# An HGRN2 recurrence with a PReLU network on one core: the first four steps as 735 single operations in a new order, and the usual steps without their column product

## The chip, the core and the metric

The kernel runs on one core of a Trainium2 chip. A core has TensorE (PE in the profile, with PEld for its weight loads), VectorE (DVE), ScalarE (ACT), GpSimd (POOL) and SyncE (SP), each with its own list of instructions, worked off in order and held up by semaphores. Data comes from HBM through DMA engines; a transfer is issued by SP, ACT or POOL, and an issue that waits holds up whatever stands behind it on that engine. The metric is the device time of one execution in microseconds (us).

## What is computed

```python
def _attn_ref(q, k, v, f_logit):                    # B, H, S, D = 4, 8, 768, 48
    f = 1.0 / (1.0 + np.exp(-f_logit))
    state = np.zeros((B, H, D, D))
    for t in range(S):
        state = f[:, :, t, :, None] * state + np.einsum('bhd,bhe->bhde', k[:, :, t], v[:, :, t])
        y[:, :, t] = np.einsum('bhd,bhde->bhe', q[:, :, t], state)

def _moe_ref(x, w_in, w_out, alpha):                # x: 3072 x 384, d_ff 2048
    h = x @ w_in
    g = np.maximum(h, 0.0) + alpha * np.minimum(h, 0.0)
    return g @ w_out
```

A recurrence over 768 times gives `y` for four batches of eight heads, and a network with one hidden layer of 2048 is applied to each of the 3072 rows.

## The kernel before

**Steps.** Time is cut in six chunks of 128 (`C`), the batches in two pairs (`U` = 2), which makes 12 steps: step 0 is pair 0 in chunk 0, step 1 is pair 1 in chunk 0, step 2 is pair 0 in chunk 1, and so on. A step has three parts. `preparation` loads f, q, k and v (token `ld`), applies the sigmoid (`sg`), and makes products of neighbouring factors (`l1` to `l3`, into `kr`, `fs` and `qd`), two scans (`sc`), and scaled queries and keys (`le`, `k4`, `e2` to `e7`; in the first chunk `gk`, `nr`; `ke`, `sa`, `sb`). From chunk 1 on, the keys are turned on VectorE (`kt`) and moved by 16 transfers on SP (`km`) into `ksn`; in chunk 0 TensorE transposes them (`kp`, copied by `kc`). `attention` makes score products (`r`, `x`, in chunk 0 also `h`, in blocks of 4, 16 and 32 times), copies them under masks into `ad` (`R`, `X`, `H`), from there into `A` (`p00` to `p13`), adds products with later keys (`of`, `oc`) and the state's columns (`s00` to `s11`), updates the state (`pd`, `m0`, `m1`, in step 0 also `pz`), and multiplies `A` with values and state (`y0`, `y1`), copied by `z0`, `z1`. The output goes into the layout of the network by transfers (`mv`), in step 0 by products with `dense` (`t0`, `t1`, copied by `T00` to `T12`). `network` multiplies by `w_in` (`n`), takes the negative part on ScalarE (`g`) and the sum on VectorE (`G`), and multiplies by `w_out`: in step 0 plainly (`va`, `vb`, result `o0`, `o1`), in the others by seven half-size products instead of eight (`A1`, `B`, `C1`, `D`, `A2`, `C2`, `E`), whose sums `S0`, `S1` are taken first.

**Weights.** `w_in` and `w_out` come as 64-bit words in eight pieces each (`id`, `jd`), through five staging buffers; ScalarE makes an upper and a lower part (`ih`, `il`, `jh`, `jl`), and a 16-bit sum on VectorE joins them (`ib`, `jb`). The first network products of step 0 (`na0`: batch a, hidden columns 0 to 511) need pieces 0 and 1.

**Order.** The order of all instructions is written out: `FIRST` lists tokens `word:step` for the first four steps (network of step n beside preparation of later steps), and `USUAL` is repeated for steps 4 to 12, where a `-` is the step before and a `+` the step behind. Each engine takes its instructions in this order. A letter at the end of a token chooses the engine: V or G for VectorE or GpSimd in `elementwise` (line 211), A or V for copies, V or A for the queue of a weight load.

**The column product** (`kw`, line 641) is a product of one column of `ident` with four columns of `ksn`. It waits for all 16 key moves, so that the state products (`pd`, line 635) behind it need no such waits. Its target is the bank that the network product `n3` then overwrites (`phk` in the profile). In `USUAL` it stands ahead of `n3`, and `pd` behind `of`.

**Memory.** PSUM holds pairs of banks (`psa`, two of them) for scores, offsets, state and output, and single banks for keys, layout and network (`psn`, four). `f`, `q`, `k` have one buffer each over the steps.

```python
def keys_landed():
    to = ahead[n - 1, 3] = bank(f"phk_{i}")
    nc.tensor.matmul(to[0:1, 0:4], lhsT=ident[:, 0:1], rhs=x["ksn"][:, 0, 0:128:32], start=True, stop=True,
                     skip_group_check=True)
```

Of the kernel before, what the change touches and what calls it, by code (L numbers as in the profile page):

```python
# [33 lines left out]
ldb:0 lda:0 id3V:0 id0V:0 id5V:0 id4V:0 id1V:0 sgb:0 qcb:0 l1bV:0 l2bV:0 l3bV:0 scb:0 c0b:0 sga:0 qca:0 l1aV:0 l2aV:0 l3aV:0 krb:0 sca:0 k4bV:0 fs:0  # L34
c1b:0 c2b:0 c3a:0 kra:0 c2a:0 c1a:0 c0a:0 cgb:0 c3b:0 ih3:0 cga:0 leaV:0 lebV:0 ih0:0 C:0 bl:0 ld:1 k4aV:0 gkaV:0 gkbV:0 nrbV:0 keaV:0 kebV:0 nraV:0
r1:0 r0:0 h0:0 H0:0 il5:0 ih5:0 h1:0 il3:0 il0:0 ih4:0 H1:0 il4:0 saaV:0 sabV:0 R0:0 ib0:0 x1:0 kpa:0 x0:0 kpb:0 sg:1 kca:0 kcb:0 R1:0 X0:0 qc:1
p01A:0 p03A:0 p02A:0 p00A:0 ih1:0 l1V:1 ib5:0 id7V:0 id6V:0 jd5V:0 id2V:0 sbaG:0 s11a:0 s10a:0 sbbG:0 s11b:0 bl:1 l2V:1 X1:0 l3G:1 pzb:0 pza:0 pda:0
pdb:0 m0a:0 ofb:0 ofa:0 oc0a:0 oc1a:0 y0:0 z0V:0 t0:0 p12G:0 p11G:0 p13G:0 p10G:0 oc1b:0 oc0b:0 il1:0 sc:1 il6:0 m0b:0 ih6:0 T01A:0 T00A:0 s10b:0 y1:0
ld:2 ib1:0 jl5:0 jh5:0 T02V:0 ib4:0 ib3:0 ib6:0 na0:0 z1A:0 il2:0 ih2:0 t1:0 cg:1 c2:1 T10A:0 c1:1 c3:1 ga0:0 c0:1 ih7:0 T11A:0 T12A:0 kr:1 m1:0 jb5:0
ib2:0 jd1V:0 jd0V:0 jd4V:0 jd2V:0 jd3V:0 leV:1 r0:1 r1:1 na2:0 nb2:0 jl1:0 jl0:0 ga2:0 k4V:1 gkV:1 saV:1 na1:0 il7:0 jl4:0 sg:2 h1:1 h0:1 H0:1 qc:2  # L40
ga1:0 Ga0:0 Ga2:0 sbV:1 ib7:0 nb0:0 jd7V:0 jd6V:0 kr:2 jl2:0 H1:1 jh4:0 gb0:0 nb3:0 gb3:0 jl3:0 jh2:0 jh0:0 nrG:1 R0:1 Ga1:0 R1:1 Gb0:0 keV:1 Gb3:0
x1:1 x0:1 nb1:0 kp:1 X1:1 X0:1 l1G:2 s10:1 l2G:2 l3G:2 k4G:2 p03G:1 s11:1 p01G:1 p13G:1 p11G:1 p02G:1 p12G:1 p10G:1 c1:2 c2:2 gb1:0 gb2:0 jh1:0 kc:1
Gb2:0 r1:2 pd:1 of:1 na3:0 c3:2 m0:1 oc0:1 oc1:1 p00A:1 c0:2 R1:2 y0:1 jb4:0 fs:1 jb1:0 jb0:0 jb2:0 jh6:0 jl6:0 jh7:0 y1:1 r0:2 jh3:0 ga3:0 z0A:1
z1A:1 jl7:0 mv:1 Gb1:0 jb3:0 leV:2 e2G:2 e3G:2 ld:3 m1:1 Ga3:0 sc:2 jb7:0 keV:2 fs:2 e4V:2 jb6:0 L:0 kt:2 e5G:2 e6G:2 R0:2 e7V:2 W00V:0 va0:0 va1:0
va2:0 n0:1 vb0:0 vb1:0 sg:3 qc:3 g0:1 l1G:3 l2V:3 saV:2 sbG:2 va3:0 x0:2 x1:2 vb2:0 G0:1 n7:1 vb3:0 n6:1 km:2 pd:2 of:2 kw:2 n5:1 n3:1 X1:2 W01V:0
# [10 lines left out]
r0 R0 x0 X0 n0- g0- G0- n1- g1- G1- r1 R1 x1 X1 n2- g2- G2- kw n3- g3- G3- S0- of oc0 oc1 pd m0 n4- g4- G4- ld+ sg+ kr+ qc+ l1+ l2+ l3+ c0+ c1+ c2+  # L56
# [25 lines left out]
def kernel(  # L82
# [65 lines left out]
    nc.scalar.dma_start(out=lvl, in_=masks)  # L148
    nc.scalar.dma_start(out=om, in_=alpha)


    vs = []
    for bp in range(B // U):
        vs.append(const.tile([128, NC2, U, DM + 16], F32, tag=f"vs{bp}", name=f"vs{bp}"))
        nc.vector.memset(vs[bp], 0.0)

    kr = const.tile([128, W // 4, 4], F32, tag="kr", name="kr")
    nc.gpsimd.memset(kr[:, :, 3:4], 1.0)
    NS = G * (NB + 1) + 1
# [18 lines left out]
    nc.gpsimd.memset(ad, 0.0)  # L178
# [3 lines left out]
    nc.gpsimd.memset(A, 0.0)  # L182
# [3 lines left out]
    def constants():  # L186
        make_identity(nc, ident)
        nc.gpsimd.tensor_scalar(om, om, -1.0, 1.0, ALU.mult, ALU.add)
        nc.gpsimd.memset(mhalf, 0.0)
        for half in range(2):  # L190
            for m in range(1, NQ):
                n = NQ - m
# [4 lines left out]
        for par in range(2):  # L197
            nc.gpsimd.tensor_copy(dense[:, (2 + par) * D:(3 + par) * D], ident[:, 64 * par:64 * par + D])
# [790 lines left out]
```

## Time and profile before

| | |
|---|---|
| time, three runs | 616.82, 619.78, 620.09 us (median 619.78) |
| span of the profiled execution | 613.4 us, clock 0.999 |
| PE, PEld, DVE, ACT, POOL busy | 96%, 86%, 79%, 40%, 18% of the span |
| instructions | 18759 |

The time of the profiled execution itself is not listed beside its span; the three runs lie 3.4 to 6.7 us above that span. The page lists busy time by engine, the chain of work that ended last, and groups of equal instructions; the trace behind it also gives stretches of the span, waits by what ended them, and instructions in order of time. In a row such as `PE L717 MATMUL xt<-y,dense` stand the engine, the line, the operation, and the target and sources by the program's tile names, without buffer numbers. "x12" counts records; a 32-bit product leaves two. PE's ends are modelled.

### The profile page before, as it was taken

How to read it: one execution, taken by the hardware profiler on the slowest of the kernel's cores; microseconds unless marked ns; L12 is line 12 of the kernel's file. 1: busy time of each engine (PE TensorE's matmuls, PEld its weight loads, DVE VectorE, ACT ScalarE, POOL GpSimd, SP SyncE). 2: the span in 40 equal slices, each digit the busy share in tenths (PEclk: the TensorE clock that was granted, in tenths of full speed). 3: DMA queues.
4: the chain of work that ended last, by engine and by line, in shares of the span. 5: the costliest groups of instructions: out<-in, count | busy, mean ns of one | idle time of the engine just before them, and what ended most of it. 6: DMA issues, size and time to landing. Idle time of an engine off the chain costs nothing.

```text
span 613.4 us, 18759 instructions
## 1 busy us (share of the span) xinstructions
PE 586.4 (96%) x8042; PEld 526.6 (86%) x8042; DVE 485.3 (79%) x993; ACT 242.5 (40%) x464; POOL 109.5 (18%) x154
## 2 busy tenths in 40 slices
PE   1689899999999999999999999999999999999997
PEld 1589766898999799899899899889899889889997
DVE  7988899985588789799899799789799889762251
ACT  5887732523412352361272271361362263223110
POOL 7437566298050000000000000000000000000000
PEclk9999999999999999999999999999999999999999
DMA  8996343141002502502502502502602601201000
GB/s 272 322 337 186 103 142 53 41 136 24 14 25 45 153 10 43 158 2 49 161 1 50 159 2 47 162 2 42 168 1 39 162 11 35 47 2 27 26 1 26
DMA packets 72002, 50.40 MB, mean 82 GB/s; under 512 B 47248, under 2 KB 62480, under 8 KB 71920
## 3 DMA queue, kind: packets, MB, share of 16 engines
q1 hardware_dynamic: 64464, 38.77, 23.6%
q0 software_dynamic: 2944, 8.59, 4.8%
q10 hardware_dynamic: 4512, 1.85, 1.2%
q8 instruction: 63, 1.03, 0.8%
q14 instruction: 19, 0.16, 0.1%
HBM read 36.21 MB, written 4.72 MB: 67 GB/s over the span
## 4 chain that ended last, share of the span: by engine, by line
PE 84%; DVE 6%; ACT 3%; issue 2%; POOL 2%; DMA 2%; POOLq 0%; ACTq 0%; DVEq 0%
PE ph L763 32%; PE pc L859 10%; PE pa L859 9%; PE pe L859 5%; PE pd L859 5%; PE pb L859 5%; PE py L694 4%; PE phk L763 4%; PE qu L514 3%; PE raw L493 3%; DMA q<-in_qT 2%; PE ph L781 2%; PE state L635 2%; PE off L597 1%; DVE w_out_sb L211 1%
## 5 line engine op out<-in xcount | busy, mean ns | idle before, releaser
L763 PE MATMUL ph<-xT,w_in_sb 128*128 128x256 f32 x948 | 213.0, 382 | 0.0
L763 PEld LDWEIGHTS ph<-xT,w_in_sb 128*128 128x128 f32 x948 | 177.7, 190 | 27.0 <-issue 1.7
L769 ACT ACTIVATE neg<-ph 128x512 f32<-128x512 f32 x79 | 46.3, 597 | 146.7 <-PE ph L763 110.7
L773 DVE SCALAR_TENSOR_TENSOR gate<-neg,om,ph 128x256 f32<-128x256 f32 x158 | 67.7, 476 | 40.5 <-ACT neg L769 39.5
L731 POOL DMA_DIRECT2D xT<-y x22 | 11.9, 546 | 392.0 <-ACT y L703 392.0
L859 PE MATMUL pa<-w_out_sb,gate 128*128 128x192 f32 x352 | 61.9, 328 | 0.1
L859 PE MATMUL pc<-t,S 128*128 128x192 f32 x352 | 61.7, 329 | 0.0
L859 PEld LDWEIGHTS pa<-w_out_sb,gate 128*128 128x128 f32 x352 | 57.9, 190 | 2.0 <-DVE gate L773 1.3
L859 PEld LDWEIGHTS pc<-t,S 128*128 128x128 f32 x352 | 57.3, 190 | 0.8 <-issue 0.2
L522 DVE COPY_PREDICATED ad<-mquad,qu 128x224 f32<-128x224 int32 (+6 forms) x140 | 42.0, 300 | 9.3 <-PE qu L514 3.2
L501 DVE COPY_PREDICATED ad<-mraw,raw 128x256 f32<-128x256 int32 (+1 forms) x96 | 42.4, 441 | 7.0 <-POOL A L680 2.8
L345 ACT COPY ut<-qd 128x256 f32<-128x256 f32 (+1 forms) x52 | 32.0, 634 | 23.2 <-DVE qd L211 12.1
L211 DVE TENSOR_TENSOR ut<-ut,fs 128x512 f32<-128x512 f32 (+6 forms) x64 | 38.5, 604 | 3.3 <-POOL ut L211 2.4
L429 ACT COPY A<-q 48x512 f32<-48x512 f32 x40 | 24.7, 616 | 35.2 <-DVE q L211 31.9
L882 ACT ACTIVATE o<-pa 128x192 f32<-128x192 f32 x11 | 3.6, 330 | 76.9 <-PE pa L859 76.9
L493 PE MATMUL raw<-qd,k 48*32 48x80 f32 x1536 | 22.4, 243 | 10.3 <-DVE qd L211 10.3
L493 PEld LDWEIGHTS raw<-qd,k 48*32 48x32 f32 x1536 | 18.1, 109 | 15.7 <-issue 15.5
L680 ACT COPY A<-ad 32x256 f32<-32x256 f32 x75 | 30.1, 401 | 1.1
L859 PE MATMUL pe<-w_out_sb,S 128*128 128x192 f32 x176 | 30.5, 327 | 0.0
L859 PE MATMUL pb<-t,gate 128*128 128x192 f32 x176 | 30.4, 326 | 0.0
L859 PE MATMUL pd<-w_out_sb,S 128*128 128x192 f32 x176 | 30.4, 326 | 0.0
L694 PEld LDWEIGHTS py<-A,vs 128*64 128x64 f32 x768 | 26.0, 145 | 4.0 <-issue 2.2
(138 smaller groups left out, 894.3 us busy)
## 6 DMA issues: line engine op xcount, KB each, us to landing
w_out_raw<-in_w_out SPq DMA_DIRECT2D x8, 767.8 KB, 5.5
w_in_raw<-in_w_in SPq DMA_DIRECT2D x8, 767.2 KB, 12.1
out<-o SPq DMA_DIRECT2D x24, 192.0 KB, 2.1
f<-in_fT SPq DMA_DIRECT2D x7, 512.0 KB, 4.3
q<-in_qT SPq DMA_DIRECT2D x7, 512.0 KB, 5.2
k<-in_kT SPq DMA_DIRECT2D x7, 512.0 KB, 6.9
vs<-in_v SPq DMA_DIRECT2D x14, 192.0 KB, 6.9
ksn<-kt SPq DMA_DIRECT2D x80, 32.0 KB, 2.0
```

Of the source, the lines that this page charges most:

```text
L211: (nc.gpsimd if beside[0] else nc.vector).tensor_tensor(*a)
L345: w[f"c{r}{mark}"] = lambda r=r: nc.scalar.copy(q4()[:, gs, :, r], qdv[r][:, gs, :, 0])
L429: copy(A[halves(cc)[1], u0:u1, par * HP:(par + 1) * HP, CH * cc:CH * (cc + 1)], x["q3"][rows(par)].rearrange("p (u h c) s t -> p u h c (s ...
L493: nc.tensor.matmul(to[DB * j:DB * (j + 1), par, hp * C:hp * C + QW], lhsT=x["k"][r_, g * DB:(g + 1) * DB], rhs=qd[r_, g], start=True, stop ...
L501: nc.vector.copy_predicated(adu[:, :, :, d:4], mraw[:, d, :, d:4].bitcast(I32).unsqueeze(1).broadcast_to((128, H, NB, n_)), rv[:, :, QO[d] ...
L522: nc.vector.copy_predicated(ad[:, u, :, :, 4 * m:DB], mquad[:, lo:lo + n_].bitcast(I32).unsqueeze(1).unsqueeze(1).broadcast_to((128, 2, HP ...
L680: copy(A[s_, u, :, s_], ad[s_, u].rearrange("p r h t -> p (r h) t"))
L694: nc.tensor.matmul(to[64 * par:64 * par + 64, u, o:o + CH], lhsT=vs[bp][:, cc, u, hd * D:hd * D + 64], rhs=A[:, u, par * HP + hp, CH * cc: ...
L763: nc.tensor.matmul(ph[f][:, j * T:(j + 1) * T], lhsT=w_in_sb[:, kt, m * 128:(m + 1) * 128], rhs=x["T"][:, kt], start=(kt == 0 and j == 0), ...
L769: nc.scalar.activation(neg[f], ph[f].rearrange("p (j t) -> p j t", j=2), AF.Relu, scale=-1.0)
L773: nc.vector.scalar_tensor_tensor(gate[:, m % NH, m // NH], neg[f][:, j], om[:, m:m + 1], ph[f].rearrange("p (j t) -> p j t", j=2)[:, j], A ...
L859: nc.tensor.matmul(p[name][:, 0:DH], lhsT=of(f), rhs=by(f), start=(f == 0 and not more), stop=(f == NH - 1), skip_group_check=True)
```

## The change

1. The set-up (clears and masks), the constants, and every group of operations that used to be one token become single tokens: `several(w, name, ops)` gives `name` for all and `name.0`, `name.1`, ... for each.
2. `FIRST` is written anew with these tokens: 735 in another order. Engines are chosen anew for each elementwise operation (for example `l1b.0G`: the first factor product of half b on GpSimd, `ib0V`: a weight sum on VectorE), and loads of f, q, k, v can go to SP (V), ACT (A) or GpSimd (G). Both halves' f and q are now loaded ahead of k and v. Step 2's f and q come from SP, between weight loads; before, GpSimd issued them.
3. Three "idle" products on a cleared part of `gate` are put in (`iq.8`, `ip.11`, `ix.8`), into the banks of `qu`, `py` and `xt0`, ahead of `r1:0`, `y0:0` and `t0:0`.
4. `kw` is taken out everywhere. In `USUAL`, `pd` moves from behind `oc0 oc1` to behind `n3 g3 G3 S0`, ahead of `of`. In `FIRST`, `pd:2` and `pd:3` stand ahead of `of` too.

```diff
 USUAL = """
-r0 R0 x0 X0 n0- g0- G0- n1- g1- G1- r1 R1 x1 X1 n2- g2- G2- kw n3- g3- G3- S0- of oc0 oc1 pd m0 n4- g4- G4- ld+ sg+ kr+ qc+ l1+ l2+ l3+ c0+ c1+ c2+
+r0 R0 x0 X0 n0- g0- G0- n1- g1- G1- r1 R1 x1 X1 n2- g2- G2- n3- g3- G3- S0- pd of oc0 oc1 m0 n4- g4- G4- ld+ sg+ kr+ qc+ l1+ l2+ l3+ c0+ c1+ c2+
...
+    def several(w, name, ops):
+        w[name] = lambda: [op() for op in ops]
+        for n, op in enumerate(ops):
+            w[f"{name}.{n}"] = op
...
-            def load():
-                loads = nc.gpsimd if 0 < n <= FROM else nc.sync
-                for name, src in (("f", fT), ("q", qT), ("k", kT)):
...
+            def loads():
+                return {"A": nc.scalar, "G": nc.gpsimd, "V": nc.sync}.get(letter[0], nc.gpsimd if 0 < n <= FROM else nc.sync)
...
+        def idle(to):
+            nc.tensor.matmul(to[:, 0:128], lhsT=gate[:, 0, 0, 0:128], rhs=gate[:, 0, 0, 128:256], start=True, stop=True,
+                             skip_group_check=True)
...
+            for mark, home in (("q", lambda: got("qu", psf)[:, 0]), ("k", lambda: got("pk", psf)[:, 0]),
+                               ("s", lambda: got("state")[:, 0]), ("p", lambda: got("py")[:, 0]), ("x", first_bank)):
+                several(w, f"i{mark}", [lambda home=home: idle(home()) for _ in range(32)])
```

The new list around the places that the prediction speaks of, first from the start to the first network product, then around the keys of step 1 and the first outputs of the network (left out: "..."):

```
zi:0 ms:0 al:0 ldb.0V:0 zd:0 zf:0 zA:0 zo.0:0 zv0:0 ci:0 zo.1:0 zm:0 mr.2:0 sgb:0 l1b.0G:0 zv1:0 ldb.1V:0 lda.0V:0 iq.8:0 qcb:0 lda.1V:0 c0b:0 ch.0:0
...
sbb.1G:0 R0.0:0 nra.1V:0 kca:0 nra.0G:0 nra.2G:0 il4:0 fs:0 cd.2:0 ld.4V:1 sg:1 ld.2V:1 cq.6:0 R0.1:0 sba.1G:0 qc:1 R0.2:0 R1.2:0 R1.3:0 x1:0 co:0
x0:0 s10a:0 ch.5:0 ch.1:0 R0.3:0 X1.0:0 X0.0:0 ofb:0 ofa:0 ch.2:0 X1.1:0 id7V:0 ih4:0 l1.0G:1 il1:0 X0.1:0 oc0a:0 s11a:0 oc1a:0 l2.0V:1 pzb:0 jd3V:0
ch.6:0 X0.2:0 p01V:0 p02V:0 p03V:0 ib5V:0 pza:0 pda:0 X1.2:0 pdb:0 m0a:0 oc0b:0 oc1b:0 p13V:0 ih1:0 cq.1:0 l3.0V:1 sc.0:1 cq.4:0 l1.1V:1 p00G:0 cg:1
p10A:0 jd2V:0 sbb.0G:0 s10b:0 ib0V:0 jd5V:0 s11b:0 ip.11:0 y0:0 ix.8:0 p12V:0 z0A:0 il3:0 ib3V:0 cd.1:0 p11A:0 bl:1 m0b:0 t0:0 T00A:0 ib1V:0 T01A:0
l2.1V:1 T02A:0 c0:1 y1:0 na0:0 il2:0 z1A:0 t1:0 ...
H1.0:1 ld.0V:2 ld.2G:2 jb5V:0 H1.2:1 sg:2 H1.1:1 ...
jh4:0 X1.1:1 jd6V:0 kp:1 X1.2:1 l2.1G:2 of:1 X0.1:1 X0.2:1 Gb1.3:0 p02V:1 jh0:0 Gb1.1:0 p11V:1 p12A:1 gb3:0 Gb3.2:0 p10A:1 p03A:1 ld.1V:4 l3.1G:2
p01V:1 r1:2 oc0:1 oc1:1 na3:0 p00G:1 kc:1 pd:1 jl7:0 l3.0G:2 r0:2 m0.1:1 m0.0:1 ...
ld.0V:3 jb6V:0 L:0 ld.4A:2 Ga3.0:0 vb0:0 sg:3 fs:1 va0:0 m1.0:1 sc.0:2 fs:2 saV:2 z0A:1 va1:0 mv:1 sb.1V:2 e2V:2 vb1:0 R0.2:2 m1.1:1 e3V:2 vb2:0 vb3:0
o1:0 ke.1V:2 ke.2G:2 e4G:2 e5V:2 va2:0 R0.3:2 kt:2 e6G:2 e7V:2 km:2 x1:2 x0:2 ...
```

More of the change, by code (lines that the diff above doesn't have):

```diff
@@ L147, with piece @@
     lvl = const.tile([128, 2, DB], F32, tag="lvl", name="lvl")
-    nc.scalar.dma_start(out=lvl, in_=masks)
-    nc.scalar.dma_start(out=om, in_=alpha)
+    pieces, ahead = {}, {}
+    def piece(name):
+        return lambda fn: pieces.__setitem__(name, fn)
+    piece("zi")(lambda: nc.gpsimd.memset(gate[:, 0, 0], 1.0))
+    piece("ms")(lambda: nc.scalar.dma_start(out=lvl, in_=masks))
+    piece("al")(lambda: nc.scalar.dma_start(out=om, in_=alpha))
     vs = []
@@ new lines @@
+    for n, (half, m) in enumerate((half, m) for half in range(2) for m in range(1, NQ)):
+        piece(f"ch.{n + 1}")(lambda half=half, m=m: half_mask(half, m))
+    piece("cd.0")(lambda: nc.gpsimd.memset(dense, 0.0))
+    for par in range(2):
+        piece(f"cd.{par + 1}")(lambda par=par: nc.gpsimd.tensor_copy(dense[:, (2 + par) * D:(3 + par) * D],
+                                                                     ident[:, 64 * par:64 * par + D]))
+    piece("cq.0")(lambda: nc.gpsimd.memset(mquad, 0.0))
```

313 lines of the change are left out of this document (157 added, 156 removed).

## The prediction, before the changed kernel had run

> **What bounds the kernel now.** I read the page first, then five stretches of the span, then the waits of TensorE.
>
> ```profile
> span 613.4 us, 18759 instructions
> PE 586.4 (96%) x8042; PEld 526.6 (86%) x8042; DVE 485.3 (79%) x993; ACT 242.5 (40%) x464; POOL 109.5 (18%) x154
> PE 84%; DVE 6%; ACT 3%; issue 2%; POOL 2%; DMA 2%; POOLq 0%; ACTq 0%; DVEq 0%
> ```
>
> ```profile
> 0.00:39.32 39.32, 20.26 (x501) 17.81 (x501) 32.36 (x74) 28.22 (x59) 22.81 (x59) 1.00 0.97 309
> 39.32:64.20 24.88, 24.87 (x504) 24.09 (x500) 22.63 (x43) 21.29 (x38) 13.46 (x15) 1.00 0.74 234
> 64.20:77.08 12.88, 10.13 (x321) 8.98 (x321) 9.82 (x26) 9.34 (x18) 5.91 (x9) 1.00 0.16 58
> 77.08:199.97 122.89, 122.38 (x1534) 104.40 (x1531) 99.58 (x196) 39.64 (x74) 58.72 (x55) 1.00 0.26 62
> 199.97:613.40 413.43, 408.72 (x5196) 371.37 (x5192) 320.90 (x658) 144.00 (x277) 8.60 (x16) 1.00 0.23 58
> ```
>
> The columns are the stretch, its length, then busy time of PE, PEld, DVE, ACT and POOL, the granted clock, DMA share and GB/s. TensorE sets the end: its products are the same ones before and after, so time can only come out of its idle time. That idle time is 39.32 - 20.26 = 19.1 us until the first network product, 2.75 us between 64 and 77, 0.5 until 200, and 4.7 behind it, the tail after the last product included. VectorE is the busy one while TensorE is idle at the start: 32.4 of 39.3 us.
>
> ```profile
> PE raw L493 <- DVE qd L211: 10.3, 2, 7.1
> PE raw L553 <- DVE ut L211: 3.4, 1, 3.4
> PE state L635 <- DVE ad L538: 3.4, 1, 3.4
> PE state L635 <- issue: 1.3, 1, 1.3
> PE keys L571 <- DVE ks L211: 1.2, 1, 1.2
> PE xt L717 <- DVE y L703: 0.9, 1, 0.9
> PE py L694 <- ACT A L616: 0.7, 1, 0.7
> ```
>
> Each row is waits in us, times, longest. The first three and the last two lie in the opening, the keys near 65, and the state wait at 207, in the first usual step.
>
> **The change part by part.** *The opening.* These rows are the end of TensorE's opening chain, and the same layout product later:
>
> ```profile
> 31.41 2.36 PE L694 MATMUL py<-A,vs 128*64 128x64 f32 x32 [0.70 <-ACT A L616]
> 34.64 2.90 PE L717 MATMUL xt<-y,dense 128*128 128x128 f32 x12 [0.88 <-DVE y L703]
> 37.46 1.92 PE L694 MATMUL py<-A,vs 128*64 128x64 f32 x32
> 39.32 0.94 PE L781 MATMUL ph<-xT,w_in_sb 128*128 128x128 f32 x6
> 42.10 1.50 PE L717 MATMUL xt<-y,dense 128*128 128x128 f32 x12
> ```
>
> ```profile
> 3.71 0.63 ACT L320 ACTIVATE f<-f 128x512 f32<-128x512 f32 x1 [0.76 <-DMA f<-in_fT]
> 8.02 0.63 ACT L320 ACTIVATE f<-f 128x512 f32<-128x512 f32 x1 [2.50 <-DMA f<-in_fT]
> 21.48 1.88 DVE L501 COPY_PREDICATED ad<-mraw,raw 128x256 f32<-128x256 int32 x4
> 37.78 2.93 DVE L211 TENSOR_TENSOR w_in_sb<-w_in_sb,w_in_lead 128x768 int16<-128x768 int16 x3
> ```
>
> The new order loads f and q of both halves before any k or v, so the second sigmoid (8.02, after 2.50 us of waiting) can start near 6.9. The price is at the other end: the first factor product moves from VectorE to POOL, behind ten short POOL instructions, the 1.8 us clear of `A` among them, and comes out near 5.7, so the first half's scores do not start earlier. I walked the three lists with the before-rows' durations, taking start-to-start where instructions of one kind follow each other (1.88 / 4 = 0.47 for a near copy, 2.93 / 3 = 0.98 for a weight sum). The near copies, at 21.48 now, come out at 18.4. On VectorE, the row durations in the list ahead of the first network product sum to 36.7 us before and 34.3 after (POOL takes parts of the factors, keys and queries; VectorE takes more score copies, and combines weight piece 1 last). At the same ratio of busy time to row sum (32.36 / 36.7) that is 30.2 us busy; idle I count 1.1 at the start, 1.5 for POOL's factor and about 1 for ScalarE's half copies, 33.8 in all, against 39.32. On ScalarE the list ahead of the first output product sums to 19.6 us, against 22.1; the walk puts the state copy it waits for at 27.1. From there by the rows above: 27.2 + 2.36 (py) + 0.6 (copy) + 2.90 (xt) + 1.92 (second py) = 35.0. So ScalarE and TensorE end last, VectorE 1.2 us before them. I take 35.0 for the first network product: **-4.3 us**. Bounds: 33.5 (if VectorE's walk also held for the others) and 39.3 (no gain).
>
> *The three idle products* read a cleared part of `gate` and stand ahead of the first scores, the first output and the first layout product. Each costs at most one layout product, 2.90 / 12 = 0.24 us, in time in which TensorE waits anyway: 0. If one is late it is 0.7 us on the path for all three.
> The same 12 layout products took 2.90 us at 34.64 and 1.50 at 42.10, while the page's granted clock reads 1.00 in both stretches: TensorE ran at half rate through the whole opening. [...]
>
> *From there to the first output of the network.* The same 24.88 us of products stand between the first network product and the keys, and the weight pieces' loads and copies keep ahead of them in the walk.
>
> ```profile
> 65.44 0.63 PE L571 MATMUL keys<-ident,ks 128*128 128x128 f32 x4 [1.24 <-DVE ks L211]
> 69.95 0.51 PE L635 MATMUL keys<-vs,ksn 64*48 64x48 f32 x26 [0.45 <-issue]
> ```
>
> The keys' waits go: their factors are made on POOL in front of other work, and offsets, a score group and the last network product now stand between key products and state products, which waited for ScalarE's key copies. In place of 2.75 us I find 0.9: output products one score group behind the state products, which must be copied first. **-1.85**; bounds 0 and -2.75.
>
> *Seams that come out as ties.* Three places where the walk has less than 1 us in hand: the third network product behind ScalarE's layout copies, step 2's scores behind a factor chain that is now all POOL's, and step 2's state products behind their key moves:
>
> ```profile
> 92.69 11.54 SPq L468 DMA_DIRECT2D ksn<-kt  x16
> 107.94 0.94 PE L635 MATMUL state<-vs,ksn 64*48 64x48 f32 x64
> ksn<-kt SPq DMA_DIRECT2D x80, 32.0 KB, 2.0
> ```
>
> The 16 moves hold SP 11.54 us and land 2.0 after the last. Now there are 107.94 - 92.69 - 13.5 = 1.7 us in hand; in the new list the first output's store stands on SP ahead of them and waits for its products. Queued behind that store is only these moves, and only the state products wait for them. Each tie costs 0 to 1 us; I take **+1.5** for the three (bounds 0 and 3).
>
> *Usual steps.* The column product goes from nine steps, and the state products move ahead of the offsets and take the landing waits themselves.
>
> ```profile
> 248.77 2.86 PE L763 MATMUL ph<-xT,w_in_sb 128*128 128x256 f32 x12
> 251.56 0.20 PE L641 MATMUL phk<-ksn,ident 128*1 128x4 f32 x2
> 251.68 2.86 PE L763 MATMUL phk<-xT,w_in_sb 128*128 128x256 f32 x12
> 256.09 10.56 PE ph L763 x48
> L641 PE MATMUL phk<-ksn,ident x18: 168/168/168, 109.5 to 535.5; 128*1 128x4 f32 x18
> L641 PEldq EVENT_SEMAPHORE  x32: 51/51/51, 199.8 to 532.9; - x32
> 233.23 11.78 SPq L468 DMA_DIRECT2D ksn<-kt  x16
> 248.77:296.00 47.23, 47.23 (x663) 42.74 (x659) 41.57 (x86) 18.39 (x35) 1.07 (x2) 1.00 0.27 68
> ```
>
> From one bank's start to the next are 2.91 us, of which the 12 products take 12 x 10.56 / 48 = 2.64: the column product costs 0.27 by that, 0.20 by its own row; 0.22 x 9 = **-2.0 us**. Its waits were served 2.6 us ahead of it (last at 532.9, last product 535.5), so TensorE's queue runs that far ahead; the state products carry about twice as many, 8 x 0.051 = 0.4 us, which a bank's 2.86 us in front hides. If nothing hid them it would be 9 x (0.41 - 0.22) = +1.7: bounds -2.4 and +1.7. The keys land well before: the moves of this step end at 245 and land 2.0 later, the products are at 254. VectorE's and ScalarE's lists keep their order; state copies start 0.8 us earlier, offset copies 0.9 later, both long before the outputs. The 1.3 us at 207 shows no releaser; I leave it, with as much again either way in the range.
>
> The sum: 4.3 + 1.85 + 2.0 - 1.5 = 6.65. The span of 613.4 becomes 606.8; the median of the three runs, 619.78 (616.82 to 620.09), is 6.4 over the span, and with that the time is **613.1 us**.
>
> **The rivals.**
> *The wait moves to VectorE.* Until the first output of the network its list shrinks by only 75.2 - 72.3 = 2.9 us of rows, while TensorE is to arrive there 6 us earlier. For: VectorE is busy 9.82 of 12.88 us in the third stretch. Against: the weight pieces it combines last are wanted by the last output parts only. If it holds, 2.9 x 0.87 + 2.0 are left: 615.3.
> *The idle products do keep the clock up.* Then the opening's layout falls from 2.90 to 1.50 and its two output products from 4.28 to about 2.1: 3.6 us more, 609.5. Against: 2.36 us of outputs just ahead at 31.41 did not do it.
> *The landing waits are not hidden:* 613.1 + 2.0 + 1.7 = 616.8.
> *Slower: one queue in order.* Step 2's f load moves from POOL to SP, behind six loads, the last of which waits until ScalarE has emptied piece 7 of the first weights; ScalarE's sigmoid then holds the half copies and ReLUs queued behind it, whose banks TensorE waits for.
>
> ```profile
> f<-in_fT SPq DMA_DIRECT2D x7, 512.0 KB, 4.3
> w_in_raw<-in_w_in SPq DMA_DIRECT2D x8, 767.2 KB, 12.1
> ```
>
> With 4.3 us to land the walk has no stall but a tie; at the 12.1 us of loads that share the engines it is 7.8 us on the path: 620.9. It decides once landing takes more than about 5 us. For: 234 GB/s in the second stretch; against: few loads are in flight then in the walk. *That the order changes nothing* is out: the lists differ on every engine from the first instruction.
>
> **How the numbers follow.** Forecast 0.54, wait moves 0.20, idle products 0.07, landing waits 0.10, queue 0.09. Half a per cent, 3.1 us, is about what a measurement of this kernel can tell: faster means below 616.7, slower above 622.9. Faster: 0.54 + 0.07 + most of 0.20 + some of the 0.10 = 0.80; same 0.13; slower, the worse part of the queue case, 0.07. The forecast with its bounds spans 609 to 617; leaving out half of the idle case and the queue case, the range is 608.5 to 617.5.
>
> **What would show it.** Right: first network product near 35, its stretch to the keys again 24.9 us, outputs near 71 (77.08 now), usual steps 47.0 us (47.23 now), no product of `ksn` with `ident` behind step 1. Wrong: the first layout product in 1.5 us (clock), a sigmoid of step 2 idle for more than 2 us on f (queue), outputs waiting for weight sums (VectorE), usual steps of 47.2 or more (waits not hidden), state products at 102 idle (moves).

## The result and the profile after

The changed kernel takes 613.37 us in the median of four executions (610.39 to 614.14), the kernel before 618.91 beside it: ratio 0.9894, 95% interval 0.9851 to 0.9936. Six more executions on another chip gave 612.52 against 618.54, 0.989 (0.9843 to 0.9937). The time forecast was 613.1. The way it was reached was not right, as the profile shows.

The page of the changed kernel, span and busy times:

```profile
span 611.8 us, 18773 instructions
PE 586.3 (96%) x8030; PEld 529.4 (87%) x8030; DVE 485.1 (79%) x990; ACT 241.7 (40%) x463; POOL 110.9 (18%) x145
```

The span is only 1.6 us shorter. Every execution whose span is listed, of either kernel, took 1.73 to 2.09 us more than its span. So the profiled execution of before (613.4) took some 615.2, and was one of its quickest: 94 executions of that kernel beside the experiments have a median span of 615.85 (four slow ones are left out, here and in the table). What tells its executions apart is the mean granted clock, which mostly lies near 1.000, 0.997 or 0.994:

| mean clock | before: executions, median span | changed: executions, median span |
|---|---|---|
| 0.999 to 1.000 | 29, 613.6 | 3, 609.0 |
| 0.995 to 0.997 | 37, 615.9 | 4, 612.0 |
| 0.994 and less | 28, 618.25 | 3, 611.4 |

At the same full clock the change is worth 4.6 us of span, going by three executions of the changed kernel. The changed kernel's last three (0.986, 0.986 and 0.989) are no longer than its four in the middle row. In the one of these with a trace, e8 below, half clock is listed for 25.2 to 32.0 us; in the first profile the column reads 1.00 over the whole opening, though its layout products took 2.90 us (1.58 in e8). So these means do not count the same thing, and the last row can't be set beside the others. The profile of before had a clock of 0.999, that of after 0.997.

Busy times by stretch, after; the borders are the first network product, the keys, the first output of the network, and the first network bank of the first usual step:

```profile
0.00:37.46 37.46, 22.13 (x507) 19.25 (x507) 28.91 (x68) 26.30 (x58) 23.85 (x59) 1.00 0.92 306
37.46:62.87 25.41, 25.18 (x503) 24.46 (x501) 23.82 (x45) 23.46 (x39) 14.35 (x16) 1.00 0.81 265
62.87:77.07 14.20, 11.91 (x330) 10.65 (x321) 13.76 (x29) 9.04 (x19) 6.17 (x6) 0.88 0.17 60
77.07:199.97 122.90, 120.63 (x1483) 103.19 (x1486) 97.12 (x193) 38.99 (x73) 57.90 (x50) 1.00 0.24 56
199.97:611.80 411.83, 406.49 (x5242) 371.86 (x5227) 321.53 (x660) 143.93 (x277) 8.60 (x16) 1.00 0.24 60
```

The first network product comes 1.9 us earlier (39.32 before), but the first output of the network is where it was, 77.07 against 77.08: all of the 1.9 is given back between them. Only behind 77 does the kernel gain for good, 534.7 us to the end instead of 536.3. The longest waits of TensorE, after:

```profile
PE raw L517 <- ACT f L352: 5.5, 1, 5.5
PE raw L574 <- DVE ut L235: 2.6, 1, 2.6
PE raw L574 <- POOL ut L235: 2.3, 1, 2.3
PE raw L517 <- ACT kr L353: 2.1, 1, 2.1
PE off L617 <- issue: 1.9, 1, 1.9
PE py L730 <- DVE vs L695: 1.7, 1, 1.7
```

The two waits ahead of the near scores, 10.3 us for VectorE before, are now 5.5 and 2.1 us, for ScalarE; new are the wait for POOL and, at 113, one for a state sum of VectorE. The opening of the changed kernel, rows of TensorE, ScalarE, VectorE and POOL from the timeline:

```profile
18.15 1.08 PE L574 MATMUL raw<-ut 48*64 48x32 f32 x32 [2.29 <-POOL ut L235]
32.72 2.90 PE L753 MATMUL xt<-y,dense 128*128 128x128 f32 x12 [0.58 <-ACT y L739]
17.71 0.89 ACT L264 ACTIVATE w_in_lead<-w_in_raw 128x768 f16<-128x768 bf16 x1 [4.65 <-DMA w_in_raw<-in_w_in]
21.14 1.28 DVE L524 COPY_PREDICATED ad<-mraw,raw 128x256 f32<-128x256 int32 x3 [3.54 <-PE pk L591]
17.30 0.29 DVE L235 TENSOR_TENSOR ut<-ut,fs 128x128 f32<-128x128 f32 x1
14.45 3.65 POOL L235 TENSOR_TENSOR ut<-k,ut 128x256 f32<-128x256 f32 x1 [2.98 <-DVE k L235]
```

From the list of transfers up to 40 us, the piece that ScalarE waits for (size, and us from issue to landing):

```profile
w_in_raw<-in_w_in ACTq DMA_DIRECT2D x1, 767.2 KB, 11.1
```

The near copies stand at 21.14 (21.48 before; the forecast had 18.4). Two things are late ahead of them: one of POOL's products takes 3.65 us, and ScalarE stands until 17.71, waiting for the load of a weight piece, with the half copies behind it. The row of the near copies names a key product of TensorE, which ends at 21.13; ScalarE's last half copy ends at 21.11, so the row alone does not tell them apart. The experiments separate the two.

### The profile page after: what moved, and what is told of

Same layout as the page of the kernel before. It is cut to its first block, busy times and chain, and to the rows that moved or that the text cites. A ratio compares the mean times of both kernels' runs of the same rounds, so it can differ in the third digit from the quotient of the medians.

```text
span 611.8 us, 18773 instructions
## 1 busy us (share of the span) xinstructions
PE 586.3 (96%) x8030; PEld 529.4 (87%) x8030; DVE 485.1 (79%) x990; ACT 241.7 (40%) x463; POOL 110.9 (18%) x145
## 4 chain that ended last, share of the span: by engine, by line
PE 83%; DVE 6%; ACT 4%; DMA 3%; POOL 2%; issue 1%; SPq 0%; DVEq 0%; POOLq 0%; ACTq 0%
PE ph L799 36%; PE pc L894 10%; PE pa L894 10%; PE pd L894 5%; PE pe L894 5%; PE pb L894 5%; PE py L730 4%; PE raw L517 3%; PE qu L537 3%; DMA w_in_raw<-in_w_in 2%; PE ph L817 2%; PE state L655 1%; PE off L617 1%; DMA f<-in_fT 1%; PE xt L753 1%
## 5 line engine op out<-in xcount | busy, mean ns | idle before, releaser
L799 PE MATMUL ph<-xT,w_in_sb 128*128 128x256 f32 x1056 | 236.4, 382 | 0.0
L799 PEld LDWEIGHTS ph<-xT,w_in_sb 128*128 128x128 f32 x1056 | 198.5, 190 | 29.0 <-issue 1.5
L809 DVE SCALAR_TENSOR_TENSOR gate<-neg,om,ph 128x256 f32<-128x256 f32 x176 | 76.5, 476 | 56.9 <-ACT neg L805 56.7
L805 ACT ACTIVATE neg<-ph 128x512 f32<-128x512 f32 x88 | 51.7, 597 | 161.8 <-PE ph L799 130.1
L544 DVE COPY_PREDICATED ad<-mquad,qu 128x128 f32<-128x128 int32 (+6 forms) x140 | 41.7, 299 | 7.6 <-PE qu L537 2.1
L524 DVE COPY_PREDICATED ad<-mraw,raw 128x256 f32<-128x256 int32 (+2 forms) x96 | 41.9, 443 | 6.6 <-PE pk L591 3.5
L235 DVE TENSOR_TENSOR ut<-ut,fs 128x128 f32<-128x128 f32 (+7 forms) x61 | 36.8, 603 | 1.9 <-POOL ut L235 1.3
L368 ACT COPY ut<-qd 128x256 f32<-128x256 f32 (+1 forms) x52 | 31.3, 631 | 8.6 <-DVE qd L235 8.3
```

Source lines behind the costliest of these rows:

```text
L235: (nc.gpsimd if beside[0] else nc.vector).tensor_tensor(*a)
L368: w[f"c{r}{mark}"] = lambda r=r: nc.scalar.copy(q4()[:, gs, :, r], qdv[r][:, gs, :, 0])
L524: nc.vector.copy_predicated(adu[:, :, :, d:4], mraw[:, d, :, d:4].bitcast(I32).unsqueeze(1).broadcast_to((128, H, NB, n_)), rv[:, :, QO[d] ...
L544: nc.vector.copy_predicated(ad[:, u, :, :, 4 * m:DB], mquad[:, lo:lo + n_].bitcast(I32).unsqueeze(1).unsqueeze(1).broadcast_to((128, 2, HP ...
L799: nc.tensor.matmul(ph[f][:, j * T:(j + 1) * T], lhsT=w_in_sb[:, kt, m * 128:(m + 1) * 128], rhs=x["T"][:, kt], start=(kt == 0 and j == 0), ...
L805: nc.scalar.activation(neg[f], ph[f].rearrange("p (j t) -> p j t", j=2), AF.Relu, scale=-1.0)
```

## The experiments

Times are medians in us, each ratio is to the kernel before on the same chip.

| label | what | time | ratio, 95% interval |
|---|---|---|---|
| e1_usual_alone | before, new list of usual steps | 616.20 | 0.9975 (0.9943 to 1.0006) |
| e2_first_alone | changed, old list of usual steps | 619.98 | 1.0019 (0.9996 to 1.0043) |
| e3_k16_vector | one product from POOL to VectorE | 610.73 | 0.9886 (0.9844 to 0.9928) |
| e4_no_idle | without the three idle products | 616.87 | 0.9962 (0.9938 to 0.9985) |
| e5_scalar_order | e3, and ScalarE's list changed, one product of POOL's earlier | 611.28 | 0.9907 (0.9874 to 0.9941) |
| e6_fill | changed, 43 more idle products | 617.58 | 0.9994 (0.9965 to 1.0024) |
| e7_loads_early | changed, step 5 loaded earlier | 615.44 | 0.9965 (0.9937 to 0.9993) |
| e8_changed_again | the changed kernel | 612.52 | 0.9890 (0.9843 to 0.9937) |
| e9_idle34 | e5, 34 more idle products | 618.66 | 0.9980 (0.9949 to 1.0010) |
| e10_ports | e5, three products to VectorE | 613.59 | 0.9912 (0.9880 to 0.9944) |
| e11_loads_late | changed, step 5 loaded later | 617.15 | 1.0005 (0.9983 to 1.0026) |
| e12_order_late | e5, step 5 loaded later | 615.48 | 0.9963 (0.9928 to 0.9998) |

None is below the changed kernel by more than the intervals allow.

**The changed kernel again** (no edit).

> The changed kernel unaltered, beside runs of the kernel before on the same chip, since it had been timed four times only and its single executions differ by some us. If the result of 613.4 against 618.9 holds: ratio 0.987 to 0.993, spans 608.5 to 612.5. Theory (each execution is a fixed list plus stretches of 3.4 us at half clock, about 1.7 us each, wherever TensorE's waits come close together): the spans fall into steps by the mean clock, those at 1.000 near 608.6, those at 0.997 near 611, those at 0.994 near 613 and more. Rival: the four runs were lucky, and it is within 0.5% of before.

612.52 us. Five of the six spans fall into steps as the theory has it, 609.0 and 609.9 at a clock of 1.000, 610.6 to 612.4 at 0.997. The sixth, 610.8 at 0.989, does not fit; it is the profiled one. Its profile, with the same lists, has the first network product 1.9 us earlier than the first profile of the changed kernel:

```profile
32.76 1.58 PE L753 MATMUL xt<-y,dense 128*128 128x128 f32 x12 [0.64 <-ACT y L739]
35.56 0.71 PE L817 MATMUL ph<-xT,w_in_sb 128*128 128x128 f32 x4
```

The layout products began at the same time as above (32.76, 32.72) and took 1.58 us instead of 2.90: here the clock rose ahead of them. In this profile it reads 1.00 from 21.8 to 25.2, 0.50 from 25.2 to 32.0, and 1.00 from there until 66.1. So 1.3 us of the opening's end differ between executions of one program.

**The two parts alone.**

```diff
 USUAL (put into the kernel before: e1; taken back in the changed kernel: e2)
-... n2- g2- G2- kw n3- g3- G3- S0- of oc0 oc1 pd m0 ...
+... n2- g2- G2- n3- g3- G3- S0- pd of oc0 oc1 m0 ...
```

> The kernel before with the new list of the usual steps alone: no column product in them, state products ahead of the offsets. By the prediction's term: nine products of 0.22 us go (the first usual step keeps its own, placed in the first four steps), so eight or nine of them, -1.8 to -2.0 us against before, landing waits hidden. Rival (waits not hidden): +1.7 us, usual steps of 47.4 us or more. Null: the row of the column product overlaps its neighbours and nothing is saved, 0. One usual step of before is 47.23 us; the term says 47.0.

> The changed kernel with the old list of the usual steps (column product back, offsets ahead of the state products). By the prediction's sum the first four steps alone give -4.65 us against before (span 608.8), and the usual part would be missing: 2.0 slower than the changed kernel. Rival: nearly all of the measured gain of 5.5 us is the first four steps, and this kernel is within 0.5 us of the changed one.

Alone the usual steps are worth 1.9 us (616.20 against 618.13), alone the first four steps cost 1.9, and each interval includes no change; together they bring 5.5 to 6.0. The expectation for the usual steps came out; both values that were expected of the first four steps fell, since the parts do not add. The starts of the second and third usual step show what a step costs; the columns are start and length, before, after and e1:

```profile
239.93 0.85 PE L493 MATMUL raw<-qd,k 48*32 48x80 f32 x60
287.20 0.90 PE L493 MATMUL raw<-qd,k 48*32 48x80 f32 x62
```

```profile
241.05 0.85 PE L517 MATMUL raw<-qd,k 48*32 48x80 f32 x60
287.89 0.85 PE L517 MATMUL raw<-qd,k 48*32 48x80 f32 x60
```

```profile
244.22 0.85 PE L493 MATMUL raw<-qd,k 48*32 48x80 f32 x60
291.20 0.87 PE L493 MATMUL raw<-qd,k 48*32 48x80 f32 x60
210.73 0.33 PE L597 MATMUL off<-q,kh 48*32 48x32 f32 x6 [4.93 <-issue]
```

47.27, 46.84 and 46.98 us: the new list saves 0.3 to 0.4 a step whatever the first four steps are. In e1 it is lost again in the first usual step, whose wait without a releaser, 1.27 us before, is 4.93 there. In e2 that step loses twice:

```profile
203.21 0.19 PE L675 MATMUL phk<-ksn,ident 128*1 128x4 f32 x2 [1.40 <-DMA ksn<-kt]
209.91 0.38 PE L655 MATMUL state<-vs,ksn 64*48 64x48 f32 x10 [2.26 <-issue]
```

and in the changed kernel:

```profile
191.62 12.06 SPq L492 DMA_DIRECT2D ksn<-kt  x16
206.18 0.94 PE L655 MATMUL state<-vs,ksn 64*48 64x48 f32 x64
```

The new first four steps issue the key moves of step 4 late: until 203.7 here, until 201.5 in e2, and they land some 2 us behind the last. In e2 the column product had to wait for them until 203.2; the state products that take its place, 3 us later, need not. That is one reason why the parts do not add, 1.4 us of it. The wait without a releaser, 3.7 us longer in e1 than before, is the other, by one profile of each; it is taken up below.

**Without the idle products.**

```diff
-iq.8:0 ... ip.11:0 ... ix.8:0
```

> The changed kernel without its three idle products. By the prediction they cost and bring nothing: time within 0.5 us of 613.4, first layout products 2.90 us as before, first network product at 37.5. Rival (they keep TensorE's clock up somewhere): the opening or the stretch at 62 to 77, where the granted clock fell to 0.88, gets slower by 0.5 to 3 us. Rival (they are late): first network product 0.3 to 0.7 earlier.

616.87 us, 3.5 to 4.4 slower than the changed kernel, against the prediction; the intervals of the two ratios (0.9938 to 0.9985, 0.9843 to 0.9937) just miss each other. The layout products take 2.90 us as with them, and at a clock of 0.995 to 0.997 the median spans agree (612.3 and 612.0). But 7 of 12 executions lay at 0.993 or 0.994, with spans of 614.8 to 616.3; none of the ten with the idle products is over 612.4. By what way three products, of some 0.8 us each by their rows, do this is open; the profile of e4 shows the wait near 207 at 2.28 us and one stretch at half clock near 67.

**The late near copies.** First POOL's product alone, then ScalarE's list too.

```diff
-gkb.2G:0
+gkb.2V:0
 e5 beside it:
-... keb.0V:0 ih3:0 H0.0:0 ... saaV:0 ih5:0 ... H1.1:0 ih0:0 ...
+... keb.0V:0 H0.0:0 ... saaV:0 ... H1.1:0 ih3:0 ih5:0 ih0:0 ...
-... W01G:0 ... sb.0G:2 s11:2 s01:2 s10:2 ... g6:1 ...
+... sb.0G:2 W01G:0 ... g6:1 s11:2 s01:2 s10:2 ...
```

> One operation of the opening goes from POOL to VectorE: the factor product of the second half's half keys (ut<-k,ut, 128x256), which took 3.65 us on POOL at 14.45 while VectorE ran two-input products without a gap, and 0.42 us on VectorE before. Theory (POOL is kept from its operands until VectorE's row of two-input products ends): half scores at 15.9 instead of 18.15, near copies at about 18.8 instead of 21.14, first network product at 35.2 to 35.6 instead of 37.5, time 1.5 to 2.3 us below the changed kernel's 613.4. Rival (ScalarE's list sets the opening, as the prediction's walk had it): first network product still at 37 or later, time within 0.5 us.

> Two places of the opening part's lists, on top of the factor product moved to VectorE. First: ScalarE's exponent part of weight piece 3, which held ScalarE until 17.7 for its load, and of piece 5 go behind the half copies they stood ahead of. Theory (ScalarE in order behind a late load is what set the near copies, after the POOL operation alone moved nothing): half copies from about 16.8, near copies at about 18.6 instead of 21.2, first network product 34.3 to 34.8 instead of 36.6. Rival (other inputs of the near copies are as late): near copies still at 21, first network product still 36.6. Second: ScalarE's three copies of step 2's queries go behind a ReLU, and POOL makes these queries ahead of a weight difference. Theory: VectorE's gates follow at once instead of 4.4 us of idling, and TensorE's 1.7 us of waiting for the state sums near 112 goes. Rival (VectorE is simply full there): it stays over 1 us. Time with both as theory has it: 3 to 4 us below e3_k16_vector.

e3, rows of TensorE, VectorE and POOL, and then e5:

```profile
14.79 1.94 PE L574 MATMUL raw<-ut 48*64 48x32 f32 x64 [2.60 <-DVE ut L235]
14.91 0.41 DVE L235 TENSOR_TENSOR ut<-k,ut 128x256 f32<-128x256 f32 x1
21.20 1.27 DVE L524 COPY_PREDICATED ad<-mraw,raw 128x256 f32<-128x256 int32 x3 [3.27 <-ACT ad L582]
16.07 2.36 POOL L235 TENSOR_TENSOR ks<-kh,ps 128x256 f32<-128x256 f32 x1 [5.20 <-DVE kh L235]
```

```profile
25.73 1.01 PE L627 MATMUL off<-q,kh 48*64 48x64 f32 x13 [2.16 <-issue]
35.60 2.94 PE L817 MATMUL ph<-xT,w_in_sb 128*128 128x128 f32 x24
15.92 1.68 ACT L582 COPY ad<-raw 128x128 f32<-128x128 f32 x6 [2.86 <-PE raw L574]
17.85 1.27 DVE L524 COPY_PREDICATED ad<-mraw,raw 128x256 f32<-128x256 int32 x3
```

In e3 the half scores are in one piece, their second group 2.3 us earlier, and the near copies have not moved: ScalarE still stood until 17.78 for the same load. The theory that POOL's product set them fell. In e5 ScalarE makes the half copies at 15.92 and the near copies come out at 17.85. What held the near copies was ScalarE's list: in order, behind a load that was issued at 6.6 and landed 11.1 us later. What e5 gains there, 3.3 us, is again not gained at its end: the offsets wait 2.16 us without a releaser, and the first network product is at 35.60, 1.0 earlier than in e3. The second edit works by half: the wait at 113 (at 111 in e5) falls from 1.67 to 0.96 us and is now one for ScalarE.

The product that took 3.65 us on POOL takes 0.41 on VectorE, and in e3 POOL's next one takes 2.36 instead of the 0.63 that it had in the changed kernel. Both end 0.5 us after VectorE's unbroken row of two-input products does: that row ends with the product at 17.30 in the changed kernel (17.59, POOL 18.10) and at 17.94 in e3 (POOL 18.43). So in both profiles POOL's product came out only behind the whole row, nine VectorE products in the changed kernel; by what VectorE holds it up no row shows.

**The two engines at 58 to 71.** After, VectorE and POOL, with the network products behind them:

```profile
61.16 2.64 DVE L235 TENSOR_TENSOR kr<-f,kr 128x256 f32<-128x256 f32 x1
69.26 2.35 DVE L716 COPY A<-ad 32x256 f32<-32x256 f32 x2
61.89 2.78 POOL L235 TENSOR_TENSOR qd<-qd,f 128x512 f32<-128x512 f32 x2
68.81 2.36 POOL L235 TENSOR_TENSOR k<-k,kr 128x1024 f32<-128x1024 f32 x1
68.72 4.54 PE L817 MATMUL ph<-xT,w_in_sb 128*128 128x128 f32 x24 [0.29 <-DVE gate L828]
```

And the clock of a window, 0.52:

```profile
70.00:72.50 2.50, 2.50 (x14) 2.50 (x14) 2.32 (x4) 1.15 (x2) 1.17 (x1) 0.52 0.02 7
```

Here it is VectorE's instructions that take longer: 2.64 us for one product, and 2.35 for two copies of a form that takes 0.28 at 68.60. TensorE waits in small pieces from 62 to 69, 2.5 us in all, the clock is listed at 0.50 from 69 to 72, and 24 network products take 4.54 us (2.92 in e3, where it did not fall).

```diff
-... l2.1G:2 ... l3.1G:2 ... k4G:2 ... sc.1:2
+... l2.1V:2 ... l3.1V:2 ... k4V:2 sc.1:2
```

> e5_scalar_order with three of POOL's two-input products of step 2 moved to VectorE: two factor products (they stood beside a VectorE product of 0.65 us that took 2.69 at 58.8) and the key product (1024 wide, 2.35 us at 66.5, beside two VectorE copies of 0.28 us that took 2.35 together). Theory (whichever of the two engines starts a two-input operation keeps the other from its operands): the VectorE product falls to about 0.65 and the copies to about 0.28 each although VectorE does 2.3 us more work; the gates are 1.5 to 2 us earlier, TensorE's waits between 60 and 68 fall from 2.5 us to under 1.2, first outputs at 73.5 where no stretch runs at half clock (74.9 in e5_scalar_order with one). Rival (VectorE is the bound there by its work): the waits stay or grow, time the same or up to 1 us longer.

```profile
62.74 0.65 DVE L235 TENSOR_TENSOR kr<-f,kr 128x256 f32<-128x256 f32 x1
69.95 0.59 DVE L716 COPY A<-ad 32x256 f32<-32x256 f32 x2
70.02 1.33 PE L517 MATMUL raw<-qd,k 48*32 48x80 f32 x64 [4.60 <-issue]
```

That the three products on POOL lengthened VectorE's instructions is shown: 2.64 became 0.65, and two copies 0.59 instead of 2.35. A gain in time is not: 613.59, a ratio of 0.9912 where e5 has 0.9907. In this profile TensorE stood 4.60 us without a releaser at the very place, so what the edit is worth without that wait stays open.

**More idle products, and the wait without a releaser.** The page lists 63 loads of instructions of 16 KB on a queue of their own, for 8030 records of products: one block for 127 records, if all of them are TensorE's. The scores, offsets and state products use up that many in about 2 us (64 state products took 0.94 us at 206.18, 64 offset products 0.76 in e6).

```diff
 e6, in the changed kernel, and e9 likewise in e5 (20, 5, 8 and 2)
-iq.8:0 ... r0:0 ... h0:0 ... h1:0 ... x0:0 ... ip.11:0 ... ix.8:0
+iq.0:0 ... iq.19:0 ... ik.0:0 ... ik.4:0 r0:0 ... ik.5:0 ... ik.12:0 h0:0
+... ik.13:0 ... ik.18:0 h1:0 ... is.0:0 is.1:0 is.2:0 x0:0
+... ip.11:0 ip.12:0 ... ix.8:0 ix.9:0
```

> The changed kernel with 43 more idle products of 128x128 in the opening's waits (20 in all ahead of the first scores, then 5, 8, 6, 3, 2 and 2 ahead of the next groups). Theory 1 (TensorE runs at half rate in the opening because its waits and small products keep the activity low): the layout products take 1.5 us instead of 2.90, the two output products 1.1 instead of 2.25 and 1.98, first network product near 35 instead of 37.5. Rival: the small products between let it fall back each time, layout 2.9 as before, and what overshoots makes the opening later by up to 1 us. Theory 2 (the wait near 207 without a releaser is TensorE's next block of code coming late, just where the state and offset products use up instructions fastest): 43 more products are 86 more instructions ahead, the block ends elsewhere, and the wait goes (under 0.3 us instead of 1.95). Rival: it belongs to that place whatever the count, 1.3 us or more stays.

> e5_scalar_order with 34 more idle products in the opening, none where they need a bank in use (20 in all ahead of the first scores, 5 ahead of the second, 8 ahead of the half scores, 2 in the key products). Theory 1 (blocks of code come late where some 100 instructions or more are used up in a microsecond or two): the block ends move 34 products ahead, the waits without releaser of 2.16 us at 23.6 and of 1.75 us at 205 fall below 0.5 us each. Rival: the load of the block stands behind the weights whatever its place, and offsets or state products still wait until 25.7. Theory 2 (dense idle products hold the clock): TensorE at full rate from about 7 us through the half scores and key products, layout products 1.5 us; if the small products then let it fall, 2.9 us. First network product 33 to 34 if both hold, 35.6 as in e5_scalar_order if neither.

Granted clock in two stretches of e6:

```profile
6.80:23.80 17.00, 11.71 (x318) 10.33 (x316) 13.33 (x41) 10.69 (x27) 11.91 (x26) 1.00 0.97 320
23.80:40.90 17.10, 12.87 (x214) 11.95 (x215) 9.56 (x22) 10.07 (x23) 5.45 (x16) 0.50 0.67 213
```

The waits of e6, one ahead of idle products, one without a releaser, and the offsets of the first usual step:

```profile
24.46 1.62 PE L660 MATMUL state<-gate 128*128 128x128 f32 x6 [3.82 <-ACT w_in_sb L267]
33.83 1.52 PE L655 MATMUL state<-vs,ksn 64*48 64x48 f32 x33 [3.56 <-issue]
212.59 0.76 PE L617 MATMUL off<-q,kh 48*32 48x32 f32 x64
```

Behind dense idle products TensorE is quicker: the two groups of first scores take 0.92 and 0.91 us instead of 1.33, the half scores 0.99 and 0.67 instead of 1.08. But from 23.8, among small products and waits, the clock is listed at half (0.50), exactly where the chain of outputs and layouts would need it; the kernel is slower. Part of that is the edit itself: the idle products put into the state's bank stood 3.82 us for it. e9 has none there, and is no faster than before either. Theory 2 held: 43 products more, and the offsets at 212 run through without a wait. But such waits come up elsewhere, here at 33.8, in e9 at 17, 23, 30, 69, 114 and 308 (1.58 to 2.90 us each).

So the place of these waits moves with the count of TensorE's instructions. Beside them stand the times of the blocks, from the trace's list of DMA packets:

| profile | TensorE stops | block under way | TensorE goes on | wait |
|---|---|---|---|---|
| before | 207.27 | 205.82 to 206.85 | 208.54 | 1.27 |
| after | 207.71 | 206.43 to 208.68 | 209.66 | 1.95 |
| e1 | 205.80 | 208.10 to 209.16 | 210.73 | 4.93 |
| e6 | 30.27 | 30.94 to 32.38 | 33.83 | 3.56 |
| e11 | 208.50 | 207.40 to 208.63 | 210.08 | 1.58 |

Over the 14 profiles 54 waits of TensorE show no releaser and take 0.2 us or more; 51 of them end 1.2 to 1.7 us after the landing of such a block (the others 0.32, 0.98 and 3.34). That TensorE waits there for a block that came late is inferred from these times; no row names the block. The length differs from profile to profile: 1.95 and 1.25 us in two of the changed kernel, 0.44 in e3. Whether the loads of data beside the block make it late was tested in three kernels.

```diff
 e7:  -ld+ (step 5, on SP)   +ldG:5 behind e7G:4 (on POOL)
 e11: -ld+ (step 5, on SP)   +ldA at the same place (on ScalarE, behind the offset copies); e12: the same in e5
```

> The changed kernel with the loads of step 5 issued from POOL's queue, behind its last operation of the first four steps, instead of from SP's behind the key moves and the output stores (204.9 to 209.6). Theory (the code block of 16 KB, requested at 206.4, stands behind these loads): the loads are over by 205, the wait near 207 falls below 0.5 us, time 1.5 us lower and the spread between executions smaller. Rival 1 (the block is late of itself): 1.3 to 2.3 us of waiting stay. Rival 2: loads now among the 16 key moves make the moves late, and the state products at 206 wait for them 1 us or more.

> The changed kernel with the loads of step 5 (f, q, k, v, 1.9 MB) issued from ScalarE's queue instead of SP's, at the same place of the list: behind the copies of the offset products, so after about 211 instead of from 204.9. Theory (the 16 KB block of code that TensorE needs among state and offset products waits for these loads: in the changed kernel the transfers were full from 205 to 211 and the block came at 206.4 in 2.25 us): no transfers beside the block, the wait near 207 (1.95, 1.92 and 1.2 in three profiles) falls below 0.5 us, and the time is 1 to 2 us below e8_changed_again's 612.5. Rival (the block is asked for too late whatever else runs): 1.2 us or more of waiting stay. Danger: keys of step 5 come too late for their moves, products of step 5 near 247 wait.

> e5_scalar_order with the late loads of e11_loads_late. If the loads are the cause of the wait near 205: 1.75 us less than e5_scalar_order there, time 609 to 610.5, the lowest of all. Rival: 611 to 612, as e5_scalar_order.

The wait in e7:

```profile
210.99 0.31 PE L618 MATMUL off<-q,kh 48*32 48x32 f32 x10 [1.92 <-issue]
```

The wait in e11, and a wait behind it:

```profile
210.08 0.31 PE L618 MATMUL off<-q,kh 48*32 48x32 f32 x10 [1.58 <-issue]
224.63 0.59 PE L895 MATMUL pa<-w_out_sb,gate 128*128 128x192 f32 x2 [2.06 <-DVE gate L810]
```

The transfers of e11 in the stretch in which its first wait falls:

```profile
208.00:211.00 3.00, 1.42 (x67) 1.22 (x58) 2.93 (x6) 0.57 (x2) 0.00 (x0) 1.00 0.00 0
```

No transfer starts between 208 and 211, the block alone is still under way until 208.6, and TensorE waits 1.58 us all the same: the loads of step 5 are not the cause. Beside them the block itself took longer, 2.25 us in the changed kernel and 1.23 here. What decides when a block is started is open, and so is why e7 as a whole gains less than the changed kernel (0.9965, 0.989). e11 and e12 pay for the late loads in the way the prediction's queue rival had it, with 2.06 us at 224 in e11 and 2.08 at 220 in e12, when ScalarE and then VectorE's gates stand behind the sigmoid of a late f.

## Why the prediction came out right

*The span and the time.* "the median of the three runs, 619.78 (616.82 to 620.09), is 6.4 over the span" is a step that failed: an execution lies 1.8 over its span, another 2.45 are the profiled execution being quicker than the median of 94 (615.85), and the last 2.1 are three runs that were slower than most. With 1.8 alone the sum would have given 608.6 us. No execution of any kernel here was that short.

*The opening, -4.3.* It was 1.9 in the first profile and 3.8 in the second (39.32 to 37.46 and 35.56), 1.3 of the difference being the clock (2.90 against 1.58 us for the layout products). The step that failed is the walk of ScalarE's list, which had no wait for the load of weight piece 3, although the row of these loads, 12.1 us, stood in the prediction; e5 took that wait away and had the near copies at 17.85, where 18.4 was forecast. The walk also took POOL's products at their undisturbed length (one took 3.65 us, the next of its size 0.63). That VectorE ends 1.2 us ahead of TensorE came out: its last weight sum there ends at 36.30, the first network product starts at 37.46. In e8, where TensorE gets there at 35.56, that sum is what it waits for (36.38, products go on at 36.44).

*To the first output of the network, -1.85.* Wrong in sign: that stretch grew from 37.76 to 39.61 us, 1.6 of it by the half clock (24 network products in 4.54 us instead of 2.92), and without it (e3: 36.61 to 74.86) still by 0.5. The waits for the keys went as foreseen (0.7 us left), but TensorE is still idle for 2.29 us there (2.75 before), in pieces, 1.75 of it for VectorE's gates and copies. That POOL's products beside VectorE's make them late is not shown: in e10, with three of them moved to VectorE, the keys still wait 0.87 us for a gate.

*Three seams, +1.5.* Of the named ones step 2's scores waited 0.8 us at 66, though for VectorE's copies and not for POOL's factors, and step 2's state products not at all. In their place came 1.67 us for a state sum at 113: POOL late with step 2's queries, ScalarE standing behind them, VectorE's gates behind ScalarE. These waits are of the size forecast by chance, and the time is not there: the stretch from the first output to the usual steps takes 122.90 us, 122.89 before. TensorE is idle 1.8 us longer in it and busy 1.8 us less; why it is busy less no run separates.

*Usual steps, -2.0.* Right in mechanism, too small: nearly the same work from the second usual step's start to the last product takes 370.2 us before (239.93 to 610.10) and 367.4 after (241.05 to 608.41), 2.8 less, 0.40 in each of seven steps where 0.22 was counted. How that divides between the column product and the place of the state products no run separates. The landing waits are hidden.

*The wait at 207*, left as it was with as much again either way: 1.27 before, 1.95 and 1.25 after, none (e6) to 4.93 (e1) over the experiments.

*The idle products, 0.* The 0.24 us each are the price of one record; a product leaves two, and the rows of these show some 0.8 us. In the opening nothing shows that they cost or bring time: without them (e4) the layout products took 2.90 us too. But the sign named for the clock rival, the first layout product in 1.5 us, came in e8 (1.58), and no run tells whether the idle products have a part in it. For the median 0 was wrong, by e4.

So the sum of 6.65 met 4.6 us at equal clock, some 2 us too much. The 6.4 us from span to time were 2.5 too much: an execution of the changed kernel takes 1.8 over its span, and its median span, 611.1, lies 2.1 over the ones at full clock (609.0). The two errors cancel. As a gain, 6.7 us were forecast (619.78 to 613.1) and 5.5 and 6.0 measured. That the time fell within 0.3 us of the forecast is mostly luck; what can be kept of the forecast is its sign, its range, and the mechanism of the usual steps.

## What to carry to other kernels

Compare one profile with one profile only at the same mean clock, look where their half-clock stretches lie, and take the step from span to time from executions that list both. In a list by hand, an operation that waits for a load holds everything behind it on its engine (ScalarE stood 4.65 us here, with the half copies behind it): put what TensorE needs next ahead of it. And before work goes to POOL, look at what VectorE runs beside it: here a 128x256 product took 3.65 us on POOL where another took 0.63, and one on VectorE 2.64 where it took 0.65 in e10.

## What the runs showed of the hardware that was not expected

Among small products TensorE can stand without a releaser in the profile, for up to 4.93 us (e1). The page lists 63 loads of instructions of 16 KB for 8030 records of products, and in 51 of 54 such waits TensorE goes on 1.2 to 1.7 us after the landing of one of them. That it had come to the end of its own instructions is inferred from these times. The places moved when 34 and 43 products were put in (e9, e6), and not when the loads of step 5 were moved: ahead of the same last ten offset products it stood 1.95 us in the changed kernel, 1.92 in e7 and 1.58 in e11.

TensorE was quicker behind a row of 128x128 products: in e6, 20 idle ones fill 1.10 to 8.52, and the first scores behind them took 0.92 us (1.33 in the changed kernel). Among small ones it may or may not be: from 18.15 to 31.3 TensorE was busy but for 1.1 us in the first profile of the changed kernel, and the layout products still took 2.90; in e8, with the same lists, full clock is listed from 21.8 to 25.2 and again from 32.0, and they took 1.58. What made the two executions differ no run here shows. The clock column reads 1.00 in the opening of the first profile, beside these 2.90 us, so lengths of equal products are the better witness there.
